# Gated linear attention and a dense layer in one kernel: the layer's weights loaded in f32 on SyncE's queue and cast on chip, with a new order of the work

## The chip, the cores and the metric

The kernel runs on one core of one Trainium2 chip. The core has five engines that take their own instructions in order and wait for one another by semaphores: TensorE (PE in the profile, with its weight loads as PEld), VectorE (DVE), ScalarE (ACT), GpSimd (POOL) and SyncE (SP), which only issues DMAs here. DMAs that any of them issue are carried out by the same 16 DMA engines of the core.

The metric is the device time of one execution in microseconds, from start to end, as a median over repeated runs. Lower is better.

## What is computed

Inputs are q, k, v and alpha, each of 4 batches x 8 heads x 768 steps x 48 numbers in f32, and two weight matrices w_in (384 x 2048) and w_out (2048 x 384), also in f32 (3.1 MB each).

```
state = alpha[t] (along rows) * state + k[t] v[t]^T      # per batch and head, 48 x 48
y[t]  = q[t] state
x     = y as 3072 tokens x 384 (8 heads x 48)
h     = x @ w_in ;  g = h * cos(h) ;  out = g @ w_out
```

The output is 3072 x 384 in f32.

## The kernel before, in words

**Tiling.** The 3072 tokens are cut into 24 chunks of 128 steps; chunk j belongs to batch j // 6. Two neighbouring chunks make a group g = j // 2 of 256 tokens, which is the moving side of the dense layer. Inside a chunk the recurrence is done in parallel: with the running products of alpha (made from Ln, a matmul with a triangle of ones, and Exp), k is divided and q multiplied by them, and the chunk's output is a masked 128 x 128 product of scores with v plus the scaled q times the state before the chunk.

**The order.** The whole program is one list of units, `ORDER` (lines 17 to 45): each word is a letter and an index, and `for u in ORDER.split()` (L390) emits the unit's instructions. Every engine gets its share of that list in that order, so the list fixes what stands behind what on each engine and on SyncE's queue. These are the letters (with the lines of the kernel before):

| Letter | Unit | Engine |
|---|---|---|
| a, k, q, v | load of one chunk of an input, 196.6 KB in rows of 192 B (L158, L161) | SyncE's queue |
| w | load of a quarter of the weights, with a cast to bf16 in the DMA (L167, L171) | GpSimd's queue |
| i, l | Ln of alpha, one or two chunks (L185) | ScalarE |
| c, C | running sums by matmul, one or two chunks (L191, L193) | TensorE |
| d, E | the two Exps (icp, cp; L201, L202), one or two chunks | ScalarE |
| K; R, O | k scaled by icp (L206); q scaled by cp (L212), on GpSimd (R) or VectorE (O) | GpSimd, VectorE |
| P, M | v cast to bf16 (L216); decay factors Em (L220) | GpSimd |
| T, t | transposes of scaled k and q on TensorE (L227) and their copy out of PSUM (L232) | TensorE, VectorE |
| D | the same transposes by DMA, SBUF to SBUF (L236), in place of T and t | SyncE's queue |
| A, m | scores (L243), and their mask (L248) | TensorE, VectorE |
| S, u, b | state of the chunk (L257), its sum with the carried state (L272, or L262 for the first of a batch), its decay (L262) | TensorE, VectorE, GpSimd |
| Y, y; Q, z | outputs of one chunk, or of two (L303), and their copy to xT (L310, L321) | TensorE, VectorE |
| F, f, p; H, h, g | part of x @ w_in (L341; F: 8 blocks of w_in for one chunk, H: 4 blocks for two), cos by Sin (L347), product h cos(h) (L352) | TensorE, ScalarE, VectorE |
| V | a quarter of g @ w_out for one chunk (L362): V index = 4 x chunk + quarter | TensorE |
| e, o | copy of the result (L366) and its store (L370) | ScalarE, SyncE's queue |
| x | dummy matmuls on zeros (L375), as many as the index says | TensorE |

So A15 is the scores of chunk 15, C5 the running sums of group 5 (chunks 10 and 11), Q2 the outputs of group 2, H8 the first quarter of group 2's first layer, V8 the first quarter of chunk 2's second layer.

**Buffers.** Inputs have 6 slots each (alpha 4 of two chunks). PSUM is shared out by `Slots` (L48): three tiles of two banks named `two` (C, A, Q, F, H) and two of one bank named `one` (T, S, Y, V). A slot that is taken again makes the new user wait for the last reader of the old one. The weights stand in w1 and w2 (L129, L130) in bf16 for the whole run.

**Around the change.** In the kernel before, chunks 0 to 7 are transposed on TensorE (8 T) and chunks 8 to 23 by DMA (16 D). The q of chunks 0 and 1 is scaled on VectorE, all the rest on GpSimd. The four w stand in GpSimd's stream after the first two or three chunks have been scaled, w0 and w1 (the halves of w_in) before w2 and w3 (the halves of w_out). The dummy matmuls are 66, in nine places before the first H. Ln and Exp share one table of ScalarE, Sin needs another; `table` (L175) makes a table load at each change in the order.

Of the kernel before, what the change touches and what calls it, by code (L numbers as in the profile page):

```python
# [9 lines left out]
FP = mybir.dt.float32  # L10
BF = mybir.dt.bfloat16
AF = mybir.ActivationFunctionType
# [5 lines left out]
k1 a0 a3 a1 k0 v1 q0 a2 q2 i0 x12 c0 v3 d0 k2 M0 i1 x7 c1 k3 K0 d1 q1 K1 q3 P1 O0 x13 T0 v0 l1 t0  # L18
a5 x2 C1 E1 a4 v2 K2 q5 R2 K3 k5 x15 T2 O1 t2 T1 k4 A0 t1 q4 P0 x1 A1 w0 S1 S0 a6 u0 w1 u1 l2 M1
m0 R3 x8 C2 w2 m1 T3 E2 M2 Y0 w3 t3 A2 y0 P2 Y1 m2 b1 S2 A3 M3 P3 u2 M4 m3 b2 Q1 x6 F0 z1 y1 S3 f0  # L20
F2 p0 f2 x2 F3 p2 F1 f3 H6 p3 f1 H4 p1 h6 u3 V4 h4 g6 b3 V5 V0 g4 V1 v4 H5 a7 V2 h5 v5 R5 V3 g5 V6
a8 e0 K5 V7 a9 H7 K4 e1 q6 R4 T5 h7 V8 t5 k6 V9 g7 T4 v9 P4 V10 t4 v6 V11 l3 S4 e2 A4 q7 u4 A5 P5
C3 m4 b4 o2 V12 E3 m5 V13 k7 S5 Q2 l4 u5 M7 M6 o0 R6 C4 z2 a11 M5 K6 V14 E4 H10 v7 b5 q8 T6 P6 k8
H8 t6 h10 R7 q11 S6 a10 V15 h8 g10 K7 H9 q9 e3 u6 g8 M9 T7 k9 M8 h9 H11 t7 k10 P7 g9 V16 h11 v8 R8
S7 A6 u7 A7 o1 V17 m6 b7 V20 a13 m7 V21 V18 a12 l5 g11 Q3 o3 R9 C5 z3 v10 K8 V19 E5 H12 K9 D8 e4
R11 H14 D9 M10 P8 H13 h12 K10 o4 q10 k11 g12 S8 h13 V22 v11 V23 u8 h14 q12 g13 H15 b8 e5 P10 k12
g14 V28 M11 k13 h15 P9 S10 V29 a15 g15 V30 a14 A8 R10 l6 A9 m8 V31 v12 K11 C6 e7 m9 E6 S9 D10 P11
Q4 u9 b9 D11 V24 z4 R12 V25 u10 v13 H18 K12 v14 b10 H16 D12 h18 H19 q15 g18 h16 o5 P12 S11 g16 h19
H17 M12 v15 u11 o7 V26 g19 h17 V27 a16 P13 V32 g17 e6 M13 A10 q13 A11 m10 S12 V33 o6 l7 V34 a17
m11 C7 k14 Q5 E7 a18 u12 A12 z5 P15 V36 R15 V37 m12 K13 V38 H22 R13 M15 H20 D13 b11 h22 P14 H21  # L30
q19 g22 K14 h20 q17 q14 V35 g20 v16 h21 V39 k15 q21 e8 H23 g21 e9 o9 V40 h23 S13 V41 u13 R14 g23
A13 V44 b13 l8 D14 V45 m13 V46 K15 q20 V47 v17 C8 D15 Q6 E8 P16 q16 V42 z6 a19 e11 V43 M16 R17 k17
H24 o8 q18 P17 k16 M14 S14 a21 h24 H25 u14 b14 e10 g24 S15 h25 o10 H26 R16 k18 g25 V48 h26 K17 H27
# [33 lines left out]
def kernel(  # L67
# [10 lines left out]
    nc = tc.nc  # L78
    B, H, S, D = q.shape
    DM, DF = moe_w_in.shape  # L80
    C = 128
# [75 lines left out]
    def load(bufs, src):  # L157
        return lambda j: nc.sync.dma_start(out=bufs[j % len(bufs)], in_=rows(src, j))  # L158
# [261 lines left out]
```

## Time and profile before

| What | Value |
|---|---|
| median of 3 runs | 195.33 us (195.08 to 195.69) |
| the profiled execution's own time | 195.0 us |
| its span, first to last instruction | 192.9 us |
| busy: PE / DVE / ACT / POOL | 182.5 / 117.7 / 120.1 / 81.6 us |
| mean rate of the DMA engines | 162 GB/s over 31.23 MB |
| granted TensorE clock | 1.000 |

The profile is of one execution. Its span begins with the first instruction and ends with the last; 2.1 us of the execution's time lie outside it. The last matmul ends at 189.67 us, 3.2 us before the end of the span. "Busy" adds up the durations of an engine's instructions; in the rows of 40 slices each digit is a fortieth of the span, 4.8 us, and 9 means 90% or more. Lines of groups give the source line, engine, operation, output and inputs, count, then busy us, mean ns, and the idle time just before with what ended it. In the timeline each line is a start, a duration, and what ran.

### The profile page before, as it was taken

To read this page: it belongs to the slowest core of one execution; us is meant where nothing else is said; L and a number is where in the kernel's file an instruction comes from. 1 tells how busy PE (TensorE), PEld (TensorE's weight loads), DVE (VectorE), ACT (ScalarE), POOL (GpSimd) and SP (SyncE) were. 2 spreads that over 40 slices of the span, in tenths; PEclk is the share of its full clock that TensorE was granted. 3 is DMA by queue.
4 is the path that set the end of the run, shared out by engine and by line. 5 is a ranking of instruction groups with operands and counts; after the bars stand their busy time and mean duration, and the time that the engine had idled before them with its cause. 6 is when DMAs were issued, how large, how long until landed. Compare 5 with 4: busy or idle time off the path is not lost.

```text
span 192.9 us, 4781 instructions
## 1 busy us (share of the span) xinstructions
PE 182.5 (95%) x1990; PEld 131.8 (68%) x1994; DVE 117.7 (61%) x138; ACT 120.1 (62%) x133; POOL 81.6 (42%) x128
## 2 busy tenths in 40 slices
PE   7997889989999999997999998999999999999993
PEld 2444468957688687685777685786786786876861
DVE  5025784844847928829828438748758578596450
ACT  2540344744768668947739567789999982361632
POOL 3317950055294655571190656271239761030000
PEclk9999999999999999999999999999999999999999
DMA  6999999999989999999989999999998762200112
GB/s 127 188 187 188 146 190 188 184 196 194 190 192 176 205 233 207 188 168 196 268 162 192 175 214 218 175 227 205 149 217 158 135 152 34 85 0 3 41 41 82
DMA packets 123092, 31.23 MB, mean 162 GB/s; under 512 B 117184, under 2 KB 122304, under 8 KB 123072
## 3 DMA queue, kind: packets, MB, share of 16 engines
q1 hardware_dynamic: 120192, 27.80, 85.0%
q0 software_dynamic: 2880, 3.15, 10.1%
q8 instruction: 15, 0.25, 0.5%
q14 instruction: 5, 0.04, 0.1%
HBM read 25.17 MB, written 4.72 MB: 155 GB/s over the span
## 4 chain that ended last, share of the span: by engine, by line
PE 66%; DMA 13%; SPq 6%; ACT 4%; issue 4%; DVE 3%; POOL 2%; ACTq 0%; DVEq 0%
PE one L362 31%; PE two L341 21%; DMA w<-in_moe_w_out_dram 10%; PE two L303 6%; SPq L158 5%; PE two L243 3%; DVE g_sb L352 3%; DMA v_sb<-in_v_dram 2%; ACT c_sb L347 2%; PE two L191 2%; SPq L161 2%; ACT L347 1%; PE one L257 1%; POOL w L167 1%; PE two L193 1%
## 5 line engine op out<-in xcount | busy, mean ns | idle before, releaser
L352 DVE TENSOR_TENSOR g_sb<-two,c_sb 128x1024 bf16<-128x1024 f32 x48 | 58.0, 1221 | 27.7 <-ACT c_sb L347 27.2
L362 PE MATMUL one<-w,g_sb 128*128 128x384 bf16 x384 | 69.5, 327 | 1.4 <-DVE g_sb L352 0.8
L341 PE MATMUL two<-xT,w 128*128 128x256 bf16 (+1 forms) x624 | 68.4, 264 | 1.0 <-DVE g_sb L352 1.0
L347 ACT ACTIVATE c_sb<-two,halfpi 128x1024 bf16<-128x1024 f32 x48 | 52.6, 1113 | 19.5 <-PE two L341 19.0
L341 PEld LDWEIGHTS <-w 128*128 128x128 bf16 x624 | 56.7, 98 | 9.7 <-issue 1.1
L362 PEld LDWEIGHTS <-g_sb 128*128 128x128 bf16 x384 | 35.3, 98 | 24.0 <-DVE g_sb L352 1.7
L206 POOL TENSOR_TENSOR kqb<-k_sb,icp 128x384 bf16<-128x384 f32 x24 | 23.9, 997 | 20.5 <-DMA k_sb<-in_k_dram 12.6
L262 POOL TENSOR_TENSOR ub<-sc,Em 128x384 bf16<-128x384 f32 x20 | 16.6, 829 | 33.1 <-DVE sc L272 31.8
L248 DVE TENSOR_TENSOR A_sb<-two,mask_f 128x1024 bf16<-128x1024 f32 x24 | 28.5, 1217 | 2.6 <-PE two L243 2.6
L212 POOL TENSOR_TENSOR kqb<-q_sb,cp 128x384 bf16<-128x384 f32 x22 | 21.9, 998 | 9.4 <-DMA q_sb<-in_q_dram 5.7
L366 ACT ACTIVATE o_sb<-one 128x384 f32<-128x384 f32 x24 | 11.7, 492 | 15.5 <-PE one L362 15.5
L347 ACT ACT_TABLE_LOAD x11 | 14.1, 1283 | 9.9 <-PE two L341 6.2
L216 POOL CAST vpb<-v_sb 128x384 bf16<-128x384 f32 x24 | 12.0, 504 | 17.2 <-DMA v_sb<-in_v_dram 9.3
L375 PE MATMUL one<-warm 128*128 128x512 bf16 x62 | 17.1, 418 | 2.2 <-DVE warm L102 1.2
L185 ACT ACTIVATE lnab<-a_sb 128x768 bf16<-128x768 f32 (+1 forms) x13 | 10.3, 794 | 12.5 <-DMA a_sb<-in_alpha_dram 12.4
L201 ACT ACTIVATE icp<-two 128x768 f32<-128x768 f32 (+1 forms) x13 | 9.9, 761 | 11.8 <-PE two L193 9.0
L272 DVE TENSOR_TENSOR sc<-one,ub 128x384 f32<-128x384 f32 x20 | 11.0, 552 | 8.2 <-PE one L257 7.9
L321 DVE CAST xT<-two 128x768 bf16<-128x768 f32 x11 | 10.5, 958 | 8.4 <-PE two L303 8.4
L179 ACT ACT_TABLE_LOAD x11 | 14.1, 1283 | 0.9 <-PEq L404 0.7
L303 PE MATMUL two<-A_sb,vpb 128*64 128x128 bf16 x264 | 13.2, 220 | 0.1
L303 PEld LDWEIGHTS <-vpb 128*64 128x64 bf16 x288 | 12.8, 110 | 0.5 <-issue 0.3
L375 PEld LDWEIGHTS <-warm 128*128 128x128 bf16 x66 | 6.4, 104 | 9.6 <-issue 3.6
(42 smaller groups left out, 114.1 us busy)
## 6 DMA issues: line engine op xcount, KB each, us to landing
k_sb<-in_k_dram SPq DMA_DIRECT2D x24, 192.0 KB, 4.6
a_sb<-in_alpha_dram SPq DMA_DIRECT2D x24, 192.0 KB, 4.3
v_sb<-in_v_dram SPq DMA_DIRECT2D x24, 192.0 KB, 4.4
q_sb<-in_q_dram SPq DMA_DIRECT2D x24, 192.0 KB, 4.2
out_dram<-o_sb SPq DMA_DIRECT2D x24, 192.0 KB, 3.7
w<-in_moe_w_in_dram POOLq DMA_DIRECT2D x2, 768.0 KB, 10.0
w<-in_moe_w_out_dram POOLq DMA_DIRECT2D x2, 768.0 KB, 17.7
qkT<-kqb SPq DMA_TRANSPOSE x16, 3.8
```

Of the source, the lines that this page charges most:

```text
L179: nc.scalar.preload_act_table_set("natural_log_exp_and_others")
L206: nc.gpsimd.tensor_tensor(out=kqb[j % 4][:, 0, :, 0:D], in0=k_t[j % 6], in1=icp_t[j // 2 % 3][:, j % 2].rearrange("s (h d) -> s h d", h=H) ...
L212: eng.tensor_tensor(out=kqb[j % 4][:, 1, :, 0:D], in0=q_t[j % 6], in1=cp.rearrange("s (h d) -> s h d", h=H), op=ALU.mult)
L216: nc.gpsimd.tensor_copy(out=vpb[j % 4][:, :, 0:D], in_=v_t[j % 6])
L248: nc.vector.tensor_tensor(out=A_t[j % 4].rearrange("s (h t) -> s h t", h=H), in0=two[("A", j)].rearrange("s (h t) -> s h t", h=H), in1=mas ...
L262: eng.tensor_tensor(out=ub[j % 3][:, :, 0:96].rearrange("r p (a e) -> r p a e", a=2), in0=src.rearrange("r p (a e) -> r p a e", a=2), in1= ...
L303: nc.tensor.matmul(t[64 * half : 64 * half + 64, kt * C : (kt + 1) * C], lhsT, rhs, start=start, stop=stop, skip_group_check=True)
L341: nc.tensor.matmul(t[:, m * n : (m + 1) * n], w1[:, kk, f * C : (f + 1) * C], x_t[g % 3][:, kk, bs].rearrange("r b t -> r (b t)"), start=( ...
L347: nc.scalar.activation(out=c_s.take((name, i)), in_=two[(name, i)], func=AF.Sin, bias=halfpi, scale=1.0)
L352: nc.vector.tensor_tensor(out=g_t[g % 3][:, fs, bs], in0=shaped(two[(name, i)], name), in1=shaped(c_s[(name, i)], name), op=ALU.mult)
L362: nc.tensor.matmul(one[("o", j)][:, 0:DM], g_t[j // 2 % 3][:, f, j % 2], w2[:, f], start=(f == 0), stop=(f == NF - 1))
L375: nc.tensor.matmul((one.free or two.free)[0][:, 0:512], warm[:, 0:C], warm, start=True, stop=True)
```

## The change

It touches the weights and the order.

The weights are no longer loaded by four DMAs on GpSimd's queue that cast f32 to bf16 on the way. They come as 14 blocks in f32 on SyncE's queue (unit W, `load_piece`): blocks 0 to 5 are 128 rows of w_in by half of its columns, rows of 4 KB (524 KB each; 0, 1, 2 are the first half of the columns, 3, 4, 5 the second), blocks 6 to 13 are two row blocks of w_out, rows of 1536 B that lie one after the other in memory (393 KB each). They land in five staging tiles `wf` and are then cast to bf16 into w1 or w2 by VectorE (unit J), ScalarE (j) or GpSimd (G). F with an even index needs blocks 0 to 2, with an odd one 3 to 5, each H a part of one half; quarter n of V needs blocks 6 + 2n and 7 + 2n.

The order is another one throughout. Counted in it: 14 W, 7 J, 2 j, 5 G; 5 T and 19 D (8 and 16 before); 7 O and 17 R (2 and 22 before); a new unit B, which scales k on VectorE, 4 times, leaves 20 K; x adds to 44 in seven places. `scale_k` takes its engine as an argument. Loads of inputs, stores and all other matmuls are the same in number. Lines of the new kernel are 26 to 28 higher than before after the inserted functions.

```diff
@@ -15,33 +15,33 @@
-k1 a0 a3 a1 k0 v1 q0 a2 q2 i0 x12 c0 v3 d0 k2 M0 i1 x7 c1 k3 K0 d1 q1 K1 q3 P1 O0 x13 T0 v0 l1 t0
-a5 x2 C1 E1 a4 v2 K2 q5 R2 K3 k5 x15 T2 O1 t2 T1 k4 A0 t1 q4 P0 x1 A1 w0 S1 S0 a6 u0 w1 u1 l2 M1
-m0 R3 x8 C2 w2 m1 T3 E2 M2 Y0 w3 t3 A2 y0 P2 Y1 m2 b1 S2 A3 M3 P3 u2 M4 m3 b2 Q1 x6 F0 z1 y1 S3 f0
...
-S7 A6 u7 A7 o1 V17 m6 b7 V20 a13 m7 V21 V18 a12 l5 g11 Q3 o3 R9 C5 z3 v10 K8 V19 E5 H12 K9 D8 e4
-R11 H14 D9 M10 P8 H13 h12 K10 o4 q10 k11 g12 S8 h13 V22 v11 V23 u8 h14 q12 g13 H15 b8 e5 P10 k12
...
+k1 W0 a1 q0 a0 k0 W1 q1 v0 i1 i0 a3 a2 W2 x23 c0 c1 k2 q2 v1 d0 d1 B1 O0 K0 O1 x11 T0 W3 q3 a5 k3
+a4 t0 l1 P0 j0 P1 T1 S0 A0 t1 C1 J1 m0 J2 E1 x2 Y0 A1 W5 K2 M0 R2 y0 x1 F0 S1 m1 u0 u1 J3 O3 v2 x4
+T2 Y1 M2 t2 x2 A2 f0 l2 K3 M1 C2 T3 W4 y1 p0 m2 t3 v3 F2 b1 G5 k5 v4 P2 M3 J4 S2 E2 f2 A3 k4 W11
+q5 P3 W7 W6 q4 F1 u2 b2 m3 p2 S3 W8 f1 Q1 P4 K5 R5 G7 B4 x1 F3 z1 f3 u3 p1 p3 G11 W9 R4 b3 H4 T5
+W10 W13 h4 g4 t5 J6 J9 H7 S4 H6 H5 u4 W12 j8 h5 h6 h7 a8 D4 J10 V4 V0 V1 V2 V5 V6 a9 a7 v5 a6 g5
+G13 M4 G12 b4 g7 g6 V3 V7 e0 P5 M5 v6 o0 e1 l4 A5 A4 V12 V13 l3 m5 m4 V14 V15 C4 S5 C3 Q2 k6 k7 q7
+u5 q9 q6 V8 E3 e3 E4 z2 V9 H8 B7 B6 k9 v7 h8 P6 M7 R6 O7 K9 M6 b5 P7 V10 S6 k8 O9 g8 u6 D7 D6 q8
+a12 a13 H11 H9 V11 S7 H10 h11 h9 e2 h10 g11 u7 g9 l6 V20 O8 K8 b7 M9 D9 g10 D8 a11 V16 V21 A7 a10
+A6 M8 V17 m6 m7 v8 o1 V22 C6 V23 E6 Q3 v9 o3 A9 A8 z3 l5 V18 V19 P8 P9 C5 e5 S8 m8 m9 o2 k13 o5
+v11 H12 u8 S9 E5 b8 Q4 H15 k11 q13 q11 u9 z4 H16 h12 g12 e4 h15 H17 K13 K11 R13 h16 v10 k10 o4 v12
+q10 V24 b9 K10 P11 M10 P10 g15 h17 O11 g16 H13 H14 g17 a15 H18 D11 a14 k12 h13 g13 S10 h14 g14 u10
+P12 R10 M11 M12 b10 H19 V25 S11 h18 h19 V26 V27 u11 g18 g19 l7 e6 V36 a17 D10 V37 q12 V38 V32 C7
+A10 A11 K12 V39 V33 R12 m10 m11 q14 a16 o6 D13 V34 D12 l8 e9 E7 k14 q18 o9 v13 V35 e8 Q5 z5 A13
+A12 S12 V28 H20 P13 M13 K14 R14 m13 m12 a19 k15 o8 q15 a18 q17 k20 u12 R15 H23 V29 H21 S13 h20 g20
+h23 h21 K15 H22 D14 D15 g23 v14 v15 k16 a22 P14 h22 u13 g21 V30 C8 g22 V31 V40 V41 E8 l9 e7 V42
+A14 A15 Q6 V43 m14 z6 M15 b11 R17 M14 b13 e10 C9 V44 V45 H26 V46 V47 v17 k17 o7 o10 q19 k18 v16
+S14 E9 m15 M16 K16 P15 u14 h26 e11 g26 H27 h27 b14 P17 P16 q16 a20 S15 H24 Q7 u15 g27 z7 h24 H25
+h25 g24 H31 S16 V52 H28 g25 h31 M17 R16 R18 K17 K18 b15 h28 q20 o11 a21 u16 H29 V53 g31 g28 v19
+R19 h29 v18 D16 D17 q22 v23 a23 k22 v21 q23 v20 V48 g29 P19 M18 V54 V49 A17 A16 v22 k23 H30 V55
+b16 P18 m17 m16 l10 h30 e13 V50 Q8 V51 V60 o13 q21 C10 z8 g30 e12 E10 l11 H32 V61 S17 H34 V62 h32
...
+e20 h46 g44 H47 V88 o21 o20 g45 h47 g46 V89 V92 g47 V93 V94 V90 V95 V91 e23 e22 o23 b23 o22
@@ -148,6 +148,7 @@
     two = Slots(psum("two", [C, 1024]), 3)
     one = Slots(psum("one", [C, 512]), 2)
     c_s = Slots(lambda i: sb.tile([C, 1024], BF, tag=f"c{i}", name="c_sb"), 3)
+    wf_s = Slots(lambda i: sb.tile([C, 1024], FP, tag=f"wf{i}", name="wf"), 5)
     o_s = Slots(lambda i: sb.tile([C, DM], FP, tag=f"o{i}", name="o_sb"), 3)
 
     def rows(t, j):
@@ -172,6 +173,31 @@
                                 in_=moe_w_out[i * n * C : (i + 1) * n * C, :]
                                 .rearrange("(f p) n -> p f n", p=C))
 
+
+
+    def piece(i):
+        if i < 6:
+            kk, f = i % 3, slice(i // 3 * 1024, i // 3 * 1024 + 1024)
+            return w1[:, kk, f], moe_w_in[kk * C : (kk + 1) * C, f], 1024
+        f = 2 * (i - 6)
+        return (w2[:, f : f + 2], moe_w_out[f * C : (f + 2) * C, :].rearrange("(f p) n -> p f n", p=C),
+                2 * DM)
+
+    def staged(t, i):
+        n = piece(i)[2]
+        return t[:, 0:n] if i < 6 else t[:, 0:n].rearrange("p (f n) -> p f n", f=2)
+
+    def load_piece(i):
+        nc.sync.dma_start(out=staged(wf_s.take(i), i), in_=piece(i)[1])
+
+    def cast_piece(eng, i):
+        dst, src = piece(i)[0], staged(wf_s[i], i)
+        if eng is nc.scalar:
+            eng.activation(out=dst, in_=src, func=AF.Copy)
+        else:
+            eng.tensor_copy(out=dst, in_=src)
+        wf_s.give(i)
+
     table = [None]
 
     def lnset():
@@ -202,8 +228,8 @@
         nc.scalar.activation(out=cp_t[g][:, s], in_=t[:, 0:n, 0:CW], func=AF.Exp, scale=1.0)
         two.give(("c", j))
 
-    def scale_k(j):
-        nc.gpsimd.tensor_tensor(out=kqb[j % 4][:, 0, :, 0:D], in0=k_t[j % 6],
+    def scale_k(eng, j):
+        eng.tensor_tensor(out=kqb[j % 4][:, 0, :, 0:D], in0=k_t[j % 6],
                                 in1=icp_t[j // 2 % 3][:, j % 2].rearrange("s (h d) -> s h d", h=H),
                                 op=ALU.mult)
 
@@ -375,9 +401,11 @@
             nc.tensor.matmul((one.free or two.free)[0][:, 0:512], warm[:, 0:C], warm, start=True, stop=True)
     units = {
         "a": load_a, "k": load(k_t, k), "q": load(q_t, q), "v": load(v_t, v), "w": load_w,
+        "W": load_piece, "J": lambda i: cast_piece(nc.vector, i), "j": lambda i: cast_piece(nc.scalar, i),
+        "G": lambda i: cast_piece(nc.gpsimd, i),
         "i": lambda j: ln(j, 1), "c": lambda j: cums(j, 1), "d": lambda j: exps(j, 1),
         "l": lambda g: ln(2 * g, 2), "C": lambda g: cums(2 * g, 2), "E": lambda g: exps(2 * g, 2),
-        "K": scale_k, "R": lambda j: scale_q(nc.gpsimd, j), "O": lambda j: scale_q(nc.vector, j),
+        "K": lambda j: scale_k(nc.gpsimd, j), "B": lambda j: scale_k(nc.vector, j), "R": lambda j: scale_q(nc.gpsimd, j), "O": lambda j: scale_q(nc.vector, j),
         "P": cast_v, "M": decay,
         "T": transposes, "t": ev_transposes, "D": dma_transposes,
         "S": state, "u": ev_state, "b": lambda j: decayed(nc.gpsimd, j, sc_t[j % 3]),
```

## The prediction

> **What bounds the kernel now.** I read, in this order, the 40-slice rows of the page, the windows of equal length, the timeline of the first 45 us, the chain of work that ended last, and the DMA issues.
>
> ```profile
> PE   7997889989999999997999998999999999999993
> ...
> DMA  6999999999989999999989999999998762200112
> ...
> L375 PE MATMUL one<-warm 128*128 128x512 bf16 x62 | 17.1, 418 | 2.2 <-DVE warm L102 1.2
> ```
>
> TensorE looks full from the start, but 17.1 us of it are the dummy matmuls of L375 (unit x), nearly all before 30 us. The DMA engines are full to about 150 us. Two long resources run neck and neck, so I need a clock for each.
>
> ```profile
> 10.00:20.00 10.00, 8.32 (x79) 4.64 (x79) 3.88 (x6) 2.36 (x3) 4.77 (x7) 1.00 1.45 188
> ...
> 18.53 0.50 POOL L216 CAST vpb<-v_sb 128x384 bf16<-128x384 f32 x1 [1.23 <-DMA v_sb<-in_v_dram]
> ...
> 18.98 1.71 POOL L167 DMA_DIRECT2D w<-in_moe_w_in_dram  x2
> ...
> 29.62 1.50 PE L341 MATMUL two<-xT,w 128*128 128x128 bf16 x24
> ...
> 42.80 2.76 PE L362 MATMUL one<-w,g_sb 128*128 128x384 bf16 x16 [0.53 <-DMA w<-in_moe_w_out_dram]
> ...
> 43.40 1.00 POOL L206 TENSOR_TENSOR kqb<-k_sb,icp 128x384 bf16<-128x384 f32 x1 [1.91 <-DMA k_sb<-in_k_dram]
> ```
>
> **The DMA clock.** Between 10 and 20 us the queues move 188 GB/s (last column): one 196.6 KB input load per 1.05 us. The n-th load on SyncE's queue lands at 2.7 + 1.05n: the 2nd (a0) at 4.8, where Ln starts at 4.80; the 7th (q0) at 10.1, used at 10.15; the 15th (v0) at 18.5, used at 18.53. The loads bind the first 20 us. The 21st load, k4, should land at 24.8; it is used at 43.40. The four weight DMAs issued from GpSimd at 19 to 24 us took the other 18.5 us, about 2 of it a dip (109 and 89 GB/s in the windows 20:21 and 21:22). First MoE matmul: 29.62; the last half of w_out is still waited for at 42.80.
>
> From k4 (43.3) to the last v (used at 150.35) 74 loads, 13 DMA transposes and 16 stores land in 107 us. 74 x 1.05 = 77.7. A transpose moves 262 KB: at the 200 GB/s of this stretch 1.3 us (two of them and one load lie between v12 used at 86.14 and v13 at 90.04, so at most 1.4). A store alone takes 0.54 us of DMA share, but runs the other way beside loads; 0.25 closes the sum: 77.7 + 16.9 + 4.0 = 98.6, the rest 8.4 us of dips, which the windows show (128 GB/s at 98:100, 92 at 138:140).
>
> **The TensorE clock.** In the chain a unit H is 1.31 us (12 matmuls), F 1.34, V 0.65 (4), Q 1.24, A 0.275, S 0.17, T 0.45, C 0.52. All units but x add to 160.65 us. "Lag" below is the time minus the work already done. In the order, 27.3 us stand before C3, which ran at 51.02: lag 23.7. C5 at 68.19: 24.3. C8 at 109.22: 26.6. C9 at 123.29: 27.5. The end, 189.67: 29.0. So 23.7 of 29.0 us are lost before 51 us, and 5.3 later in small waits.
>
> **The skill.** "DMA: Bandwidth & Descriptors", Issuing engines are not separate DMA queues: DMAs from any engine share the same 16 engines; another queue saves only issue time. The trace agrees: the weights took from the loads what they moved (18.5 us). The same page, iDMA fabric, gives 408.7 GB/s for a stream of loads with 4 KiB rows; no run here shows it, the nearest row is the store (1536 B rows, 197 KB in 0.54 us, 364 GB/s). "VectorE: DVE Perf Modes", Mode 2×_2P: a one-source copy between SBUF tensors handles two elements a cycle even in f32; the trace has no such copy.
>
> **What the change removes and adds.** (1) Four GpSimd DMA issues go (1.71 + 0.94 + 0.91 us of its time at 19 to 24 us, not waited for by TensorE), and with them the dip of 2 us. (2) Fourteen loads come onto SyncE: issuing at least 0.43 us each as the shortest load, 6 us, hidden because its queue is full. On the engines, six pieces of 524 KB at 364 to 409 GB/s are 1.28 to 1.44 us, I take 1.3; eight of 393 KB are 0.96 to 1.2, I take 1.05: together 16.2, ends 15.4 to 18.2, against 16.5 before. The bytes cost the same; their place changes: W0 is second instead of last. (3) Fourteen casts. GpSimd: 0.504 us for 384 columns gives 1.34 us (G5) and four of 1.0. ScalarE: two of 0.8 to 1.1 (L185 to L347). VectorE: seven of 0.6 (two a cycle) to 1.2 us (one), I take 0.7; 5 us. They lie before 45 us, where VectorE idles half the time (2.57, 3.88 and 4.55 us busy in 10, 10 and 5). Without that cover each is up to 1.2 us before an F or V. (4) Five more q-scalings and four k-scalings on VectorE at 0.67 to 1.25 instead of GpSimd's 1.0: 6 to 11 us on an engine that has 75 free; as they stand ahead of gates (g8 behind O9), one may cost 0.5. Minus three copies of 0.69. (5) T falls from 8 to 5: TensorE 159.3 instead of 160.65, a gain of 1.35; three more DMA transposes cost 3.9 us of the DMA clock. (6) x falls from 66 to 44: no cost unless TensorE slows down when it idles, as it seems to at the start (the first 12 took 4.80 us, 13 later ones 2.97); the granted clock was 1.00 in every window, and by my sums no new gap passes 2 us. (7) Table switches of ScalarE fall from 22 to 18, 5 us off an engine that isn't the bound; TensorE can gain part of 1.28 where a gate waits (84.63).
>
> **New waits.** wf has five slots, so W4 waits for j0, W11 for J1, and so on to W12 for J6; behind a waiting W stand all loads. [...] a cast late by under 6 us costs nothing; W10 (G7 at about 37) and W13 (G11, 38) come near.
>
> **The sum, prologue.** SyncE's new order with this clock: a0 8.2, W2 16.1, v1 19.2, a4 24.7, W4 28.4, q4 37.8, W12 43.0, D4 45.4, v5 48.5, a6 49.6. TensorE: F0 at 18 to 19 instead of 29.6. But T2 waits for k2, q2 and GpSimd, held in order by P1 (v1): 22. C2 waits for a4, F1 for W4: 29. Q1 ends at 32, while before it ended at 28. T5 waits for q5 and R5, V3 for W12 and its cast (44.9). C3 waits for a6 and Ln: 50.7, then Q2 to 52.4 with 29.3 done: lag 23.1. Before, at the end of its Q2, 54.4, it was 23.8. So the eleven microseconds by which F0 starts earlier are nearly all given back, because the same bytes must land before Q2.
>
> **The sum, after it.** The new order puts attention earlier: A15 has 80.1 us of work before it, 93.2 before the change. So DMA comes due earlier. Landings: a13 65.0; Ln and C6 (41.3 done): lag 24.7. a10 69.7, C5 (45.6): 25.1. D12 95.3, A12 (68.9): 26.4. D15: 69 loads 72.4, weights 16.2, 11 transposes 14.3, 9 stores 2.3, start 2.7: 107.9; A15: lag 27.8. After that 27 loads stand against 79 us of work (k19 would need only 26.9). I add 1.3 for small waits to the end, as C9 to the end before (1.5), less for the switches. TensorE ends at 159.3 + 27.8 + 1.3 = 188.4, against 189.67. Evacuation, store and what lies outside the span stay 3.2 + 2.1 us: 193.7 against the profiled execution's own 195.0. The median of the runs is 195.33, so 194.0.
>
> **Rivals.** *Loads keep ahead:* from k4 to v5 (used at 43.4 and 48.09) five loads took 0.95 each. At that price the 53 loads after 20 us save 5.3; D15 lands at 102.6 and no longer binds. Lag is 23.1 plus 3.2 of small waits: 185.6, total 191.2. Against it: eight pure loads from q10 (77.4) to v12 (86.14) took 1.09 each. *The transposes bind (slower):* if one occupies the queue for its median issue time, 1.62 us, instead of 1.3, eleven of them put D15 at 111.4, A15's lag at 31.3, the end at 191.9, the total at 197.5. The waits of SP for L236 below speak for it, the 3.9 us between v12 and v13 against it. It decides from D15 landing after 109.8: then TensorE ends after 190.3 and the total passes 195.9. *It does nothing:* the casts come so late that the order of F and V is that of before; only T's 1.35 is left, less the 1.3 of one gate delayed: 195.3.
>
> ```profile
> qkT<-kqb SPq DMA_TRANSPOSE x16, 3.8
> ...
> SPq L236 <- POOL kqb L206: 9.6, 5, 2.3
> ```
>
> **Chances.** DMA binds at A15 with the prices above: 0.45, from 192.6 to 195.7. Loads ahead: 0.25. Transposes bind: 0.25. Nothing: 0.05. I take 0.3% (0.6 us) as about what a measurement here can tell from no change. Faster: 0.33 of the first and the second, 0.58; same: 0.12 + 0.03 = 0.15; slower 0.27. The bounds of the weights (15.4 to 18.2) move A15 by -0.8 to +2.0. The range 190.6 to 197.8 reaches to both rivals.
>
> **What would show it.** F0 before 20 us; all weights cast by 45; Q2's end within 1 us of 52.4; TensorE waiting at C6 or C5 for a13, a10, and at A12 or A15 for qkT from DMA, lag 28 there. Wrong if TensorE is full from 53 us on (then 191), if D15 lands after 110, if a VectorE cast takes over 1.2 us, or if the granted clock falls.

## The result and the profile after

The changed kernel takes 206.45 us (median of 4 runs, 204.86 to 207.62) against 195.26 us (195.08 to 195.69) before it: a ratio of 1.056, with a 95% interval of 1.049 to 1.064. It is slower. The forecast was faster, 194.0 us, and its range ended at 197.8. Here and below, the few executions that took over 1.5% longer than the fastest of their kernel are left out. The profiled execution took 207.62 us, the longest of the four, with a span of 205.8.

From the page of the changed kernel, the 40-slice rows and the first line of the chain of work that ended last, and below it the same line of the kernel before:

```profile
PE   7697499798897789989989899989986999999992
...
PEclk9969889999999999999999999999997899999999
DMA  6999998999999999898999999999996143110012
...
SPq 31%; DMA 23%; PE 23%; POOL 8%; issue 5%; DVE 5%; ACT 3%; POOLq 0%; ACTq 0%
```

```profile
PE 66%; DMA 13%; SPq 6%; ACT 4%; issue 4%; DVE 3%; POOL 2%; ACTq 0%; DVEq 0%
```

In the page of before the PE row had two digits under 9 between slice 11 and the last; now there are gaps up to slice 31 (154 to 160 us). The chain is the clearest change: TensorE's share of it was 66% and is 23%, while SyncE's queue (SPq: the issue of loads and transposes) and DMA make up 54%. So the program's end hangs on the queue of DMAs, not on TensorE. The clock row has dents (slices 3, 5, 6, 31 and 32); before, the granted clock was full throughout.

The waits of GpSimd's cast of v and of ScalarE's Ln for their loads (total us, times, longest), first in the changed kernel:

```profile
POOL vpb L242 <- DMA v_sb<-in_v_dram: 46.7, 10, 9.7
...
ACT lnab L211 <- DMA a_sb<-in_alpha_dram: 26.1, 8, 5.1
```

and in the kernel before:

```profile
ACT lnab L185 <- DMA a_sb<-in_alpha_dram: 12.4, 3, 7.4
...
POOL vpb L216 <- DMA v_sb<-in_v_dram: 9.3, 7, 3.2
```

The consumers of v and alpha now stand waiting for their loads.

Two tables of equal stretches, 54 to 154 us. Columns: stretch, its length, busy time (and instructions) of PE, PEld, DVE, ACT and POOL, then PEclk, DMA share and GB/s. First the kernel before, then the changed one:

```profile
54.00:74.00 20.00, 19.84 (x232) 15.50 (x227) 11.70 (x13) 14.42 (x17) 13.14 (x19) 1.00 1.07 198
74.00:94.00 20.00, 19.00 (x209) 13.81 (x208) 15.66 (x17) 15.45 (x17) 9.24 (x15) 1.00 1.19 203
94.00:114.00 20.00, 20.00 (x232) 14.91 (x231) 10.44 (x12) 12.14 (x15) 10.46 (x15) 1.00 1.15 195
114.00:134.00 20.00, 19.12 (x215) 14.36 (x214) 13.48 (x14) 16.73 (x18) 10.03 (x15) 1.00 1.29 204
134.00:154.00 20.00, 20.00 (x238) 14.60 (x233) 13.86 (x13) 19.33 (x22) 10.47 (x17) 1.00 0.90 171
```

```profile
54.00:74.00 20.00, 15.83 (x180) 11.41 (x179) 12.05 (x15) 12.57 (x15) 6.30 (x12) 1.00 1.16 181
74.00:94.00 20.00, 18.86 (x235) 15.25 (x233) 14.01 (x16) 14.94 (x17) 10.55 (x16) 1.00 1.08 219
94.00:114.00 20.00, 18.36 (x204) 13.17 (x202) 13.35 (x14) 11.66 (x14) 6.54 (x8) 1.00 1.03 199
114.00:134.00 20.00, 19.07 (x230) 14.86 (x229) 10.22 (x11) 13.37 (x17) 11.42 (x18) 1.00 1.10 200
134.00:154.00 20.00, 18.44 (x196) 13.19 (x194) 13.28 (x14) 16.86 (x19) 8.31 (x14) 1.00 1.18 195
```

The last column says that the queue moves data no slower than before: 199 GB/s on average against 194. TensorE does 90.6 us of work in these 100 us instead of 98.0. The same stream of data carries less of TensorE's work: the question is what stands in the stream, and when TensorE asks for it.

TensorE's last wait for the stream is at A19 and A18 (start, duration, idle time before and its releaser):

```profile
157.12 0.80 PE L269 MATMUL two<-qkT 48*128 48x128 bf16 x16 [2.04 <-DMA qkT<-kqb]
157.86 4.22 PE L388 MATMUL one<-w,g_sb 128*128 128x384 bf16 x16
```

Here 116.0 us of TensorE's work stand before A19 in the order, so the lag is 41.1 us. In the kernel before the same pair of scores started at 147.09 without a wait and with 119.1 us done, a lag of 28.0:

```profile
147.09 0.62 PE L243 MATMUL two<-qkT 48*128 48x128 bf16 x16
```

After A19 no wait is left that matters: 45.0 us for 43.3 us of work. The second line is a consequence of the first: sixteen matmuls of V that take about 2.7 us took 4.22, because the clock had fallen (0.57 on the mean of 157 to 160 us) after the idle time.

### The profile page after: what moved, and what is told of

Same layout as the page of the kernel before. It is cut to its first block, busy times and chain, and to the rows that moved or that the text cites. A ratio compares the mean times of both kernels' runs of the same rounds, so it can differ in the third digit from the quotient of the medians.

```text
span 205.8 us, 4719 instructions
## 1 busy us (share of the span) xinstructions
PE 180.2 (88%) x1945; PEld 130.2 (63%) x1948; DVE 124.7 (61%) x151; ACT 115.9 (56%) x131; POOL 73.7 (36%) x120
## 4 chain that ended last, share of the span: by engine, by line
SPq 31%; DMA 23%; PE 23%; POOL 8%; issue 5%; DVE 5%; ACT 3%; POOLq 0%; ACTq 0%
SPq L159 17%; PE one L388 11%; PE two L367 8%; DMA v_sb<-in_v_dram 7%; SPq L162 7%; DMA q_sb<-in_q_dram 5%; DMA a_sb<-in_alpha_dram 5%; SPq L262 4%; POOL kqb L238 3%; POOL kqb L232 3%; DMA qkT<-kqb 2%; SPq L191 2%; DMA k_sb<-in_k_dram 2%; DVE g_sb L378 2%; DMA out_dram<-o_sb 2%
## 5 line engine op out<-in xcount | busy, mean ns | idle before, releaser
L388 PE MATMUL one<-w,g_sb 128*128 128x384 bf16 x384 | 71.1, 331 | 1.3 <-DVE w L198 0.4
L367 PE MATMUL two<-xT,w 128*128 128x256 bf16 (+1 forms) x624 | 69.1, 264 | 3.1 <-DVE g_sb L378 1.4
L378 DVE TENSOR_TENSOR g_sb<-two,c_sb 128x1024 bf16<-128x1024 f32 x48 | 57.4, 1218 | 17.7 <-ACT c_sb L373 17.5
L388 PEld LDWEIGHTS <-g_sb 128*128 128x128 bf16 x384 | 36.4, 99 | 24.3 <-issue 3.4
L232 POOL TENSOR_TENSOR kqb<-k_sb,icp 128x384 bf16<-128x384 f32 x20 | 19.9, 1001 | 18.4 <-DMA k_sb<-in_k_dram 10.0
L211 ACT ACTIVATE lnab<-a_sb 128x768 bf16<-128x768 f32 (+1 forms) x13 | 10.3, 794 | 26.2 <-DMA a_sb<-in_alpha_dram 26.1
L238 POOL TENSOR_TENSOR kqb<-q_sb,cp 128x384 bf16<-128x384 f32 x17 | 17.0, 1000 | 9.2 <-DMA q_sb<-in_q_dram 7.7
L401 PE MATMUL one<-warm 128*128 128x512 bf16 x41 | 13.4, 478 | 3.2 <-DVE ub L288 1.4
L217 PE MATMUL two<-lnab,triu_bf 128*128 128x384 bf16 x24 | 7.0, 324 | 6.0 <-ACT lnab L211 5.9
L269 PE MATMUL two<-qkT 48*128 48x128 bf16 x192 | 8.3, 221 | 4.5 <-DMA qkT<-kqb 2.7
```

The lines of the kernel that those rows point to most:

```text
L232: eng.tensor_tensor(out=kqb[j % 4][:, 0, :, 0:D], in0=k_t[j % 6], in1=icp_t[j // 2 % 3][:, j % 2].rearrange("s (h d) -> s h d", h=H), op=A ...
L238: eng.tensor_tensor(out=kqb[j % 4][:, 1, :, 0:D], in0=q_t[j % 6], in1=cp.rearrange("s (h d) -> s h d", h=H), op=ALU.mult)
L367: nc.tensor.matmul(t[:, m * n : (m + 1) * n], w1[:, kk, f * C : (f + 1) * C], x_t[g % 3][:, kk, bs].rearrange("r b t -> r (b t)"), start=( ...
L378: nc.vector.tensor_tensor(out=g_t[g % 3][:, fs, bs], in0=shaped(two[(name, i)], name), in1=shaped(c_s[(name, i)], name), op=ALU.mult)
L388: nc.tensor.matmul(one[("o", j)][:, 0:DM], g_t[j // 2 % 3][:, f, j % 2], w2[:, f], start=(f == 0), stop=(f == NF - 1))
L401: nc.tensor.matmul((one.free or two.free)[0][:, 0:512], warm[:, 0:C], warm, start=True, stop=True)
```

## The lag, step by step

The chunk's transpose by DMA (D) is the last thing on the queue before A. So for each D one can add up what the queue has to carry before it, with the prediction's own prices (1.05 us a load, 1.3 a transpose, 0.25 a store, 2.7 at the start, weights 16.5 before and 16.2 after), and subtract TensorE's work before the A. By these prices, that difference is the least lag that the queue allows. Beside it stands the lag that the trace shows:

| At | before: loads, D, stores ahead | queue less work | measured lag | changed: loads, D, stores ahead | queue less work | measured lag |
|---|---|---|---|---|---|---|
| A9 | 47, 1, 4 | 16.7 | 24.1 | 40, 3, 1 | 21.3 | 31.6 |
| A12 | 58, 4, 5 | 17.0 | 26.2 | 60, 8, 7 | 25.1 | 35.0 |
| A15 | 73, 7, 9 | 14.0 | 27.6 | 69, 10, 9 | 26.5 | 36.8 |
| A19 | 89, 11, 14 | 11.4 | 28.0 | 96, 14, 15 | 25.6 | 41.1 |

Before, the queue had 7 to 17 us in hand and could afford its dips. In the changed order it has none: 96 loads (all of them) and three more transposes stand ahead of D19, and less of TensorE's work stands before A19 to cover them. I computed this number for A15 in the prediction (27.8 with D15's own transfer), found that it binds, and took it as the lag itself. What comes on top of it at A19, 41.1 - 25.6 = 15.5 us, is 1.3 for D19 itself, 4.9 for the weights and 9.3 that is left, below.

## The experiments

All times are medians; the interval is that of the ratio to the kernel before, run beside it (195.1 to 195.5 us).

| Kernel | us | ratio, 95% interval |
|---|---|---|
| changed kernel | 206.45 | 1.049 to 1.064 |
| new order, weights by GpSimd (first try) | 209.21 | 1.069 to 1.079 |
| new order, weights by GpSimd, earlier | 207.99 | 1.063 to 1.068 |
| old order, f32 weights | 203.50 | 1.037 to 1.048 |
| new start, old rest | 199.33 | 1.016 to 1.021 |
| new start, old rest, weights loaded twice | 222.08 | 1.133 to 1.142 |
| old start, new rest | 200.43 | 1.022 to 1.027 |
| changed, q loads halved | 197.50 | 1.006 to 1.012 |
| changed, an eighth of the weights' bytes | 195.20 | 0.997 to 1.001 |
| changed, three transposes on TensorE, late | 203.30 | 1.036 to 1.042 |
| changed, three transposes on TensorE, early | 207.57 | 1.057 to 1.070 |
| changed, ten staging tiles | 205.52 | 1.043 to 1.056 |
| changed, ten tiles, f32 blocks grouped | 209.30 | 1.066 to 1.081 |
| changed, more dummies | 205.34 | 1.045 to 1.054 |
| old order, f32 weights, more dummies | 203.54 | 1.037 to 1.047 |
| old order, f32 weights early | 199.03 | 1.018 to 1.021 |
| the same, more dummies | 198.37 | 1.012 to 1.016 |
| before, chunks 6 and 7 by DMA | 201.55 | 1.030 to 1.035 |
| before, chunks 4 to 7 by DMA | 201.09 | 1.028 to 1.032 |

### Order or weights?

My theory, A, was that both cost, through the one queue. The rivals were B, that the path of the weights is all of it, and C, that the order is all of it. First the new order alone, with the weights by the four casting DMAs:

```
-k1 W0 a1 ... W1 ... W3 ... W7 ... W10 ...     (W, J, j, G)
+k1 w0 a1 ...        w1 ... w2 ... w3  ...     (no W, J, j, G)
```

> The new order alone: the weights come as before by four casting DMAs from GpSimd, put at the places of W0, W3, W7 and W10; no f32 staging and no casts. Theory A (both parts cost, through the one DMA queue: the new order makes loads and transposes come due earlier, and the f32 blocks take some 22 us of it instead of 18.5): the queue gets 4 to 6 us back, 201 to 203 us. Theory B (the weights' new path is the whole cost): 194 to 196 us. Theory C (the order is the whole cost): 205 to 207 us.

It took 209.21 us. But this was partly my placing: the last DMA stood behind other work of GpSimd, and TensorE waited for it (start, duration, idle time before):

```profile
52.00 2.40 PE L388 MATMUL one<-w,g_sb 128*128 128x384 bf16 x7 [5.79 <-DMA w<-in_moe_w_out_dram]
```

So once more with the four DMAs at the places of W1, W3, W5 and W4:

> The new order alone once more, with the four casting DMAs issued earlier (at the places of W1, W3, W5 and W4), because in the first try the last of them stood behind other work of GpSimd until TensorE waited 5.8 us for it. Theory A (the order costs much by itself: it puts attention earlier, so the same stream of loads is late against it): 202 to 206 us. Theory B (the weights' path is the cost and the first try was slow only by the late last DMA): 195 to 199 us.

207.99 us, above the range of A, and B has fallen: the order is slow with the old path too. In it the f32 weights are not the worse path; the medians differ by 1.5 us in their favour, at intervals that just overlap. At C4 the lag is 32.7 us here and 26.7 in the changed kernel: TensorE stood 3.5 us at S1 for v1's cast, which had waited 9.2 us for v1, and from 39.5 us 4.1 us ahead of H4 for a copy on VectorE, which stood behind the scaling of k4 and its wait of 3.8 us for that load. I take it that GpSimd's DMAs overtake loads that this start waits for; that wasn't tried apart.

Then the new path of the weights alone, in the old order (ten staging tiles; the casts ahead of F0, F3, V4 and V2):

```
-... A1 w0 S1 S0 a6 u0 w1 u1 ... C2 w2 ... Y0 w3 ... x6 F0
+... A1 W0 W1 W2 S1 S0 a6 u0 W3 W4 W5 u1 ... C2 W6 W7 W8 W9 ... x6 j0 J1 J2 J3 W10 W11 W12 W13 F0
```

> The new path of the weights alone: the order of before, with the fourteen f32 loads on SyncE's queue where the four GpSimd DMAs stood and the fourteen casts ahead of the F and V that need them; ten staging tiles, so that no load waits for a cast except the last four. Theory A: 4 to 6 us more for the weights, part of it in the slack of the queue, 198 to 200 us. Theory B: 205 us or more. Theory C: 195 to 196 us.

203.50 us, 8.2 more than before: above A's range and short of B's. All of it is lost by C3: lag 31.3 there instead of 23.7, and from there to the end 5.3 us more, as before (5.3). The reason is not a slow stream. The f32 blocks as one run move at the rate that I had assumed (columns as above, the last is GB/s):

```profile
30.00:32.00 2.00, 0.23 (x1) 0.10 (x1) 0.63 (x1) 1.67 (x2) 0.00 (x0) 1.00 1.10 357
32.00:34.00 2.00, 0.79 (x6) 0.61 (x7) 0.76 (x2) 0.00 (x0) 0.00 (x0) 0.51 1.07 393
34.00:36.00 2.00, 2.00 (x22) 2.00 (x21) 1.05 (x2) 0.00 (x0) 0.00 (x0) 0.50 1.02 389
```

But on SyncE's queue they stand behind all loads up to q4. In the kernel before, k5, k4 and q4 gave way to GpSimd's DMAs: SyncE's issue of the two k took 10.01 us and that of q4 5.38 us, and TensorE needed none of them before 43 us. The first F ran on from 33.5 instead of 29.6 us. So each part costs by itself (12.6 and 8.2 us), but the two don't add: together they cost 11.2.

### Two halves

C4 lies near the end of the start, when all weights are cast. I joined the changed kernel up to C4 with what is left in the old order, and the reverse.

```
+ORDER = new order up to "C4", then the units not yet done, as in the old order
```

> The changed kernel up to C4 (all f32 loads and casts are done by then), and from there the units that are left in the order of before. If the order after 53 us is the larger part (theory A: there the new order makes every attention step wait for the loads, 16 us of lag against 5): C4 at 53.5 as in the changed kernel, then some 5 us more of lag, 197 to 199 us. If the first 53 us, with the f32 weights, are the larger part: 203 to 206 us.

It took 222.08 us, and says nothing on the question: I had left w0 to w3 in the rest, so that GpSimd loaded the weights a second time and TensorE stood still for 19.6 us. The reverse half:

```
+ORDER = old order up to "C4" (w0 to w3 in it), then the units not yet done, as in the new order
```

> The reverse: the kernel before up to C4, with the weights by its four casting DMAs, and from there the units that are left in the new order. Theory A: C4 at 54.4 with a lag of 23.8, then the new order adds 14 to 16 us: 203 to 206 us. If the first 53 us are the larger part: 196 to 198 us.

200.43 us: the new order after C4 costs 5.3 us by itself. The time lies between the two ranges expected. From C4 to the end the lag grows by 11.9 us (24.0 to 35.9), before by 5.2. And the first half mended:

```
-(the rest) ... w0 ... w1 ... w2 ... w3 ...
+(the rest) ... without them
```

> The changed kernel up to C4 and the order of before from there, now without the four casting DMAs that the first version of it wrongly kept (it loaded the weights twice). The reverse half, old start and new rest, gave 201.1 us, so the new order after C4 is worth about 6 of the 11 us. If the two halves add: 195.3 + 5.3 = 200.6 us, with C4 at 53.5 and a lag that grows by about 5 us from there. If the f32 start only hurts together with the new rest: 196 to 198 us. If the old order of the rest is as slow on this start: 204 us or more.

199.33 us against 195.51 beside it: the new start costs 3.8 us (C4's lag is 27.4 instead of 23.8, and C5's 30.0). The halves make 3.8 + 5.3 = 9.1 of the 11.2 us; the four runs of the changed kernel alone spread over 2.8. Neither "the start" nor "the rest" is the larger part by far.

### What binds the rest

If the pace of the queue binds, bytes taken from it must come off the clock one to one; if SyncE's in-order waits for scalings bind, they must not. From chunk 6 on, this kernel loads four of eight heads of q (scores of the others are of old q):

```
+        n = H if j < 6 else H // 2
+        nc.sync.dma_start(out=q_t[j % 6][:, 0:n], in_=rows(q, j)[:, 0:n])
```

> The changed kernel with only four of eight heads of q loaded from chunk 6 on (the other heads keep old values, so scores of those heads are of old q). It takes 18 times about 0.5 us, 9 us, from the DMA queue and changes no wait, no cast and no order. If the queue's pace binds TensorE from C4 to A19: A19 starts 6 to 9 us earlier than 157.1, 198 to 201 us. If TensorE waits for scalings, stores and transposes that SyncE handles in order, whatever the bytes: 204 to 206 us.

197.50 us: 18 half loads, 9.4 us of queue by the prediction's price, took 8.9 us off the clock. A19 moved from 157.12 by as much:

```profile
148.25 0.90 PE L269 MATMUL two<-qkT 48*128 48x128 bf16 x16
```

No cast or place in the order had changed, and from C4 to the end the lag grew by 6 us instead of 16. That is the queue's pace, shown.

The weights' bytes, with an eighth of each block loaded (the products are of other weights):

```
-        nc.sync.dma_start(out=staged(wf_s.take(i), i), in_=piece(i)[1])
+        nc.sync.dma_start(out=dst[..., 0:128 or 0:48], in_=src[..., 0:128 or 0:48])
```

> The changed kernel with one eighth of the weights' bytes: each f32 load fetches 128 of 1024 columns or 48 of 384, the rest of the staging tiles is zero, so the products are of other weights; order, casts and everything else stay. It prices the fourteen loads: v5 was used at 53.5 us. If they take 1.15 us each as predicted, v5 comes at 40 to 42; if 1.6 us each, at 33 to 36. If the DMA queue binds TensorE up to D19 (theory A), the end follows by nearly as much until TensorE itself binds: 187 to 193 us. If TensorE is held by casts, scalings or its clock instead: 200 us or more.

195.20 us, above the 187 to 193 expected. C4 comes at 45.0 with a lag of 18.1, yet it grows by 12.9 us to the end, as it does with all the weights in "old start, new rest" (11.9). This says most about the change: with seven eighths of the weights' bytes gone, its order is only as fast as the kernel before with all of them. The price of a block couldn't be read here: v5 came at 43.8, but SyncE waited in this kernel for casts and for the tiles' first filling.

Three transposes fewer on the queue (T4 t4, T6 t6, T7 t7 on TensorE instead of D4, D6, D7). My first places for them, after H7 and u6:

```
-H7 ... D4 ... u6 D7 D6
+H7 T4 t4 ... u6 T7 t7 T6 t6
```

> The changed kernel with chunks 4, 6 and 7 transposed on TensorE (T, t) instead of by DMA (D), as in the kernel before. Theory A (the DMA queue binds up to D19): three transposes of 1.3 to 1.6 us leave the queue, TensorE's 1.35 us more do not count: 202 to 203 us. If the transposes cost more than their bytes because SyncE holds all later loads until K and R are done, more: 200 to 201. If the weights alone or the clock alone are the cost: 206 to 208 us.

207.57 us, no gain. TensorE, in order, stood at T7 for K and R while H and its gates behind it were ready; the gates held a scaling on VectorE, and that held SyncE at a transpose (start, us):

```profile
61.66 12.31 SPq L263 DMA_TRANSPOSE qkT<-kqb  x2
```

For these 12.3 us no load went out. With the transposes just ahead of A5 and V16:

```
-D4 ... A5 A4 ... D7 D6 ... V16 V21 A7
+T4 t4 A5 A4 ... T7 t7 T6 t6 V16 V21 A7
```

> The changed kernel with chunks 4, 6 and 7 transposed on TensorE, this time just ahead of A5 and of V16, where K and R are long done (in the first try TensorE stood still at T7 for K and R, and the gates and scalings behind it held SyncE 12.3 us at a transpose). If three DMA transposes cost the queue 1.3 to 1.6 us each and the waits of SyncE for K and R besides: C6 starts 4 to 7 us earlier than 73.0 and the time is 200 to 203 us. If only their bytes count and the rest is idle anyway: 204 to 206 us. If transposes are no part of the cost: 206 to 208 us.

203.30 us, 3.2 less than the changed kernel, about 1 us for each; with the spread of both kernels it is anything from 0.5 to 1.6, so this run doesn't settle the price. C6 itself did not come earlier (75.0), so the gain lies later; the end came at a lag of 37.5 instead of 42.8.

More staging tiles, so that none of the first ten blocks waits for a cast:

```
-    wf_s = Slots(lambda i: sb.tile([C, 1024], FP, tag=f"wf{i}", name="wf"), 5)
+    wf_s = Slots(lambda i: sb.tile([C, 1024], FP, tag=f"wf{i}", name="wf"), 10)
```

> The changed kernel with ten staging tiles instead of five, nothing else: the first ten f32 loads wait for no cast. SyncE waited 7.5 us for casts between 32 and 48 us. If these waits left the DMA engines idle, v5 and a6 land 3 to 5 us earlier and the time is 202 to 204 us. If [...] the f32 blocks themselves are slow: 205.5 to 207 us.

205.52 us, and C4 at 53.9: the waits of SyncE for casts were not the cost. Within the interval this is no change.

### Blocks among the loads

By v5 (used at 53.47) 27 loads, one transpose and all fourteen blocks have landed. 53.4 - 2.7 - 27 x 1.05 - 1.3 = 21.1 us for the blocks, 1.5 each instead of 1.16. (The same remainder was 18.5 before, with the dip of 2 us in it.) The landing time of each DMA, which the trace also holds, agrees: the steps from what stood before a block on the queue to the block itself add to 21.0 us. The issue rows of SyncE show the start of it (start, time in issue):

```profile
6.63 0.75 SPq L191 DMA_DIRECT2D wf<-in_moe_w_in_dram  x1
7.43 0.43 SPq L159 DMA_DIRECT2D q_sb<-in_q_dram  x1
7.91 0.81 SPq L159 DMA_DIRECT2D v_sb<-in_v_dram  x1
8.76 4.10 SPq L162 DMA_DIRECT2D a_sb<-in_alpha_dram  x2
```

After a block, SyncE stands for 2.4 to 4.1 us at one or two of the next loads. A dip follows the first two times (6 to 7 us: 128 GB/s; 12 to 13 us: 90), after the later ones hardly. Grouped in three runs (only what is on the queue is shown):

```
-k0 W1 q1 v0 ... v1 W3 q3 a5 k3 a4 W5 v2 W4 ... k4 W11 q5 W7 W6 q4 W8 W9
+k0 W0 W1 W2 q1 v0 ... v1 W3 W5 W4 q3 a5 k3 ... k4 W11 W7 W6 W8 W9 W10 W13 W12 q5 q4
```

> The changed kernel with ten staging tiles and the f32 blocks in three runs (three behind k0, three behind v1, eight behind k4) instead of one between every two or three input loads; the 10-tile kernel without it took 205.5 us. In the order of before, blocks in one run moved at 370 to 420 GB/s, 1.26 us each, while among the loads they took 1.6 us each. If the mixture costs: by C4 the queue is 3 to 5 us ahead, C4 at 49 to 51, 201 to 203 us. If it doesn't: C4 at 53 to 55, 205 to 206 us.

209.30 us, against 205.52 for the ten tiles alone. While the run of eight passed (36 to 44 us) the queue moved 350 GB/s, 1.12 us a block of w_out, but the loads behind a run come late by its whole length, and TensorE waited for q5 and its scaling:

```profile
46.72 0.61 PE L253 MATMUL one<-ident_bf,kqb 128*128 128x128 bf16 x4 [4.23 <-POOL kqb L238]
```

So inside a run a block is cheaper, and I found no place for the runs that uses it. How much a run saves can be read at equal contents: 23 loads and all fourteen blocks had landed at 48.1 us in the changed kernel, at 46.4 here, at 46.0 in the old order with f32 weights and at 47.0 in the same with the blocks early (further down). Less 2.7 and 23 x 1.05 that is 21.2, 19.6, 19.2 and 20.1 us for the blocks; 23 loads and the four casting DMAs of the kernel before were in at 45.1, which leaves 18.2. So the mixture costs one or two microseconds, and in runs, too, the blocks take three or four more than 16.2. The steps from landing to landing show why: the first one or two blocks of w_in in a run come 2.0 to 3.5 us after what stood before them, and only those behind at about the prices that I had assumed (1.26 to 1.41 us, and 1.05 for w_out). That the mixture is what makes a block dearer rests on these kernels alone; one in which only that differs was not tried.

### The clock

The changed kernel with 27 more dummies where TensorE idled before its clock fell:

```
-x23 ... S1 ... x4 ... A19
+x31 ... x5 S1 ... x8 ... x10 A19
```

> The changed kernel with 28 more dummy matmuls where TensorE stood idle before its clock fell to 0.5: 31 instead of 23 at the start, 5 before S1, 8 instead of 4 before T2, 10 before A19. If the lower clock is a cost of its own: 1.4 us at the last waits for D19, and up to 2 in the first 30 us: 203 to 205 us. If TensorE waits for the DMA in any case, the slow stretches are absorbed by the next wait except the last: 205 to 206.5 us.

205.34 us, against 206.45: the intervals overlap. After A19 the slow V was gone (45.0 us became 43.4), so that piece is on the path. The four runs of the changed kernel point the same way: the one with the highest mean clock, 0.991, took 204.86 us, the three at 0.974 and 0.975 took 206.07 to 207.62. The old order with the f32 weights, where TensorE idled ahead of F0:

```
-Q1 x6 j0 J1 J2 J3 W10 W11 W12 W13 F0
+Q1 x24 j0 J1 J2 J3 W10 W11 W12 W13 F0
```

> The order of before with the f32 weights (203.5 us) and 24 instead of 6 dummy matmuls ahead of F0, where TensorE stood idle for 3.3 us and then worked at a clock of 0.5 from 32 to 38 us. If the clock costs what half speed over 6 us of work should: C3 starts 3 us earlier than 58.7, 200 to 201.5 us. If the weights alone hold TensorE there: 203 to 204 us.

203.54 against 203.50: nothing, though the half-speed stretch of 32 to 38 us was gone. F0 and the units after it waited for the next blocks instead. By these two runs, whether a slow stretch costs depends on whether a wait follows it.

### Candidates

The old order with the first ten f32 blocks from right after the 18th load on, ahead of k4 and q4 and in part of q5 and k5, the last four after q4, and F0 and F2 ahead of Q1 in place of eight dummies:

```
-a4 v2 K2 q5 R2 K3 k5 ... q4 ... w0 ... w1 ... w2 ... w3 ... Q1 x6 F0
+a4 v2 W0 W1 W2 K2 R2 K3 W3 W4 W5 ... q5 k5 ... W6 W7 W8 W9 k4 q4 ... F0 ... F2 Q1 ... W10 W11 W12 W13 a6
```

> A candidate: the order of before, with the f32 weights as one stream right after the 18th load, ahead of k4, k5, q4, q5 and a6, which are not used before 43 us; ten staging tiles; the first casts on ScalarE and VectorE as soon as they land, F0 and F2 ahead of Q1 in place of dummies. W2 lands at about 26 us, all weights at 43, F0 starts at 27 instead of 29.6 us. If the start is what the f32 weights cost in the old order (a matter of their place): C3 1 to 2 us earlier than the 51.0 of before, 193 to 195 us. If blocks of f32 on the queue of the loads cost more in themselves: 197 us or more.

199.03 us, where 193 to 195 was hoped for; this recovers 4.5 of the 8.2 us. F0 began at 25.7 but had all its weights only at 29.5 us, and the first V ran at 42.4 instead of 38.2. With sixteen dummies ahead of F0 (x16 F0 in place of F0):

> The candidate of before (199.0 us; old order, f32 weights as early runs) with 16 dummy matmuls ahead of F0, where TensorE idled 3.5 us and then worked three microseconds at a clock of 0.5. F0 and F2 took 4.4 us there instead of 2.7. If the clock is a cost on this path: 197 to 198 us. If the next wait absorbs it, as in the same trial on the old order with late weights: 198.5 to 199.5 us.

198.37 us, 0.7 less; the intervals do not touch. At last, two kernels with more transposes by DMA in the old order:

```
-... q8 T6 P6 k8 H8 t6 ... M9 T7 k9 ... t7
+... q8 D6 P6 k8 H8    ... M9 D7 k9 ...        (and, in the second, D5 and D4 for T5 t5 and T4 t4)
```

> The kernel before with chunks 6 and 7 transposed by DMA instead of TensorE (D6 and D7 at the places of T6 and T7), nothing else. In the changed kernel every microsecond on the queue was one on the clock (halved q loads: 9 us off both). If that is so because of its order, and the order of before leaves the queue slack after 51 us: TensorE saves 0.9 us, 194.2 to 194.9 us. If transposes by DMA cost the queue and TensorE in any order: 196.5 to 198 us.

> The same with chunks 4 to 7. If the old order has slack on the queue here as well: TensorE saves 1.8 us, 193.3 to 194.5 us. But chunks 4 and 5 are due at 47 to 50 us, four to seven microseconds after their loads, and a DMA transpose needs some 4 us to land: if it comes late, 195.5 to 198 us.

201.55 and 201.09 us. Both are above their ranges. They do not tell what I asked of them, since the way of a single transpose decides them. In the first, SyncE stood at D7 from 62.83 to 65.83, and A7 waited for it (TensorE's rows, then the clock):

```profile
63.35 0.40 PE L243 MATMUL two<-qkT 48*128 48x128 bf16 x8
67.74 0.61 PE L243 MATMUL two<-qkT 48*128 48x128 bf16 x8 [3.99 <-DMA qkT<-kqb]
68.28 4.02 PE L362 MATMUL one<-w,g_sb 128*128 128x384 bf16 x12
```

```profile
67.00:73.00 6.00, 5.26 (x23) 2.54 (x24) 2.35 (x2) 0.00 (x0) 2.70 (x3) 0.50 1.08 223
```

The lag rose from 23.8 at C4 to 31.3 at C5, where before it rose by 0.5: 4.0 us of wait and about 3 at half clock. In the second, TensorE stood 3.5 us at A4, and the lag was 5 us above that of before at C3. No kernel tried beats the one before.

## Why the prediction was wrong, step by step

**The failed step: "D15: 69 loads 72.4, weights 16.2, 11 transposes 14.3, 9 stores 2.3, start 2.7: 107.9".** D15 landed at 116.9, nine microseconds late, and the lag at A15 was 36.8 instead of 27.8. Of the nine, 4.9 are the weights (below). For the other 4.1 the sum has nothing, though I had found 8.4 us of dips in 107 us of the kernel before (9.4 if counted rightly: the v used at 150.35 is v20, and one load lands after it). By A19 they are 41.1 - 25.6 - 1.3 - 4.9 = 9.3 us, in the 104 since v5. They are not dips alone, as the landing times of the trace show. The 69 loads add 4.3 to their price: nine of them land 1.6 to 2.7 us after the transfer before, the others 0.97 on the mean. The 15 stores add 4.6: they take 0.56 each, where 0.25 had been fitted to close a sum. Thirteen transposes took 1.12 each, 2.3 less than priced. And D19 landed 4.0 us after the transfer before it, 2.7 more than its price: k19 was in at 151.0, but its scaling (1.0 us) and the way of D19 from issue to landing (5.0 us) still stood before A19, with hardly anything left on the queue to fill the time (21 GB/s in 154:156). The other emptiest stretch, 70:72 with 28 GB/s, follows 4.4 us in which SyncE stood at D9 and D8.

In the kernel before, the same count from k4 to D19 leaves 7.3 us in 98, about the same share, and 6.5 of it are the stores. There it cost nothing, because the queue had 7 to 17 us in hand. The change spent that reserve, and all such time then counts. That the queue binds there is shown (halved q loads); what each late load comes from was not tried apart.

**The same step behind A15: "27 loads stand against 79 us of work".** All 27 are due by D19. Up to there they stand against 35.9 us of TensorE's work (116.0 - 80.1), and with 4 transposes and 6 stores they take 35 us of the queue by the prediction's prices. So nothing lost could be made up. I had allowed 1.3 us from A15 to the end; the lag grew by 6.0, 4.3 of it by A19 and 1.7 after it, most of that the slow V.

**The second failed term: the weights, 16.2 us.** They took 21.1, above my bound of 18.2 (17.3 by its own rate, as 393 KB at 364 GB/s are 1.08 us and not 1.2). My rate of 364 to 409 GB/s holds for blocks inside a run (357 to 393 measured, 420 at best), not for the first of a run and not between loads of short rows. Casts late by some microseconds cost nothing, as I had said (ten tiles: no change).

Nine microseconds at A15 and 6.0 - 1.3 = 4.7 after it are the 13.7 by which TensorE's end moved (202.1 for 188.4).

**Right:** F0 before 20 us (19.52); but the last cast ended at 48.9, not by 45, and Q2 at 57.3, not near 52.4. "The eleven microseconds by which F0 starts earlier are nearly all given back" was too mild: Q2 and C3 came later than before. The order: attention stands earlier (A15 with 80.1 us of work before it), so DMA comes due earlier, and C6, C5, A12 and A15 wait. I priced that as a lag of 27.8 and called it a gain, as it lay below 29.0; the order was the cost I had named and under-measured. VectorE's casts: 0.68 us for 1024 columns, near the 0.6 for two elements a cycle (the Trainium skill, "VectorE: DVE Perf Modes", Mode 2×_2P) and far from the 1.2 for one. Casts and scalings hid on VectorE as I had said: TensorE's longest waits for it were 1.38 us (at 24 us, where VectorE itself stood behind v1's late cast on GpSimd) and 1.20 us (at 38 us).

**The rivals.** "The transposes bind (slower)" had the right place, D15 landing after 109.8 (A15 ran at 116.9), and the wrong cause: thirteen transposes landed 1.12 us each after the transfer before them, not 1.62. "Loads keep ahead" fell with the first stretches after 54 us. "It does nothing" fell too.

**The clock.** I had said that no gap would pass 2 us. In the changed kernel it fell to 0.50 at 11 to 14 us and to 0.57 in 24 to 28 and 157 to 160 us. Only the last is surely on the path (4.22 us for 2.7). The rest stays open: the run with more dummies was 1.1 us faster in all, within the spread of the runs.

## What to carry to other kernels

For each step that waits for a shared in-order queue, write down the queue's work ahead of it less the engine's work ahead of it, for every such step to the end, before and after the change: the largest of these is the lag, and what the old order had below its real lag is the reserve that hid the queue's dips. A new order that spends this reserve has to be charged with the dips of the kernel before, not with an unbroken stream, and with the whole way of the last transfer where nothing is left to hide it. A price that was fitted to close a sum should be read from the landings instead. A price measured for a transfer in a run of its like does not hold between transfers of another shape, and putting a transfer on the queue of the others takes away its chance to overtake them.

## What the runs showed of the hardware

- One wait of TensorE of 4.0 us for a DMA cost about 7 us in all, as the clock was 0.50 for the next six microseconds (chunks 6 and 7 by DMA). The Trainium skill, "TensorE: Matmul & The Clock Gate", Part 1: The HAM clock gate, says that the array runs at half rate after an idle window of about 3.4 us; this run agrees. In the changed kernel it also fell after shorter gaps near one another (0.64 and 2.04 us within six microseconds, at 157 us), which that statement alone does not give.
- Blocks of 4 KB rows in one run reached 420 GB/s over 26 to 30 us (old order, f32 weights early), and with those of w_out 357 to 393 in the old order with late weights. The prediction's figure of 408.7 from the Trainium skill, "DMA: Bandwidth & Descriptors", iDMA fabric, stands there for one core's stream with the other core of the pair idle. It is met inside such a run; over whole stretches of blocks between short-row loads no run here came near it.
- Between v5 and D19 of the changed kernel, thirteen DMA transposes landed 1.12 us each after the transfer before them on the queue, and fifteen stores 0.56 us each. With the queue empty, D22 and D23 landed 3.1 to 3.2 us after SyncE began them, and o22 and o23 1.9 us.
